# First batch of a three-layer kernel: norms, residue, Newton's steps and mix moved by slots

## The chip, the cores and the metric

The kernel runs on one core of a Trainium2 chip. The metric is the device time in microseconds (us) of one execution; of the kernel before there are three such times, and their median is what a change is held against.

## The reference, cut to what matters

Three layers follow each other: a Nyström attention (8 batches, 8 heads, 576 positions, 64 columns a head), a mixing layer with an MLP, and a Fourier mixing layer with an MLP. The change touches the attention of the first batch.

```python
q_lm = q.reshape(B, H, 32, 18, D).mean(axis=3)      # landmarks, k_lm alike
A, Bm, C = sm(q, k_lm), sm(q_lm, k_lm), sm(q_lm, k)  # softmax of scaled products
Z = Bm.T / (norm1(Bm) * norminf(Bm) + 1e-06)
for _ in range(6):
    Z = 2 * Z - Z @ Bm @ Z                           # Newton's steps
x = A @ Z @ C @ v
u = x + (x.T @ U @ V).T                              # mixing
y = u + relu(u @ w_ch1) @ w_ch2                      # MLP, float64 weights converted on the chip
```

## The kernel before, in words

Everything is written out in a hand-made order, and each engine works through its own list in that order: an instruction that waits holds up all that stand behind it on its engine. What is recorded first comes first.

Before the first MLP there are 21 slots, from `FIRST` = -21 to -1. In each slot the loop runs the steps of the batches that are due in it (`slots.run`), then perhaps `filler(s)`, then some pieces of the weights' conversion (`convs`). A batch's steps and the slots, counted from its own start, are in `Batch.steps`. Batch 0 starts at slot 0 of the 21, batch 1 eleven slots later, so batch 1's `kernel` to `query` lie beside batch 0's `heads`, `rank` and `mix`. Steps of one slot stand in the order of the batches: batch 0's first.

- `landmark` sums 18 rows of k or q on VectorE and scales them into `kb` and `qb`. `landmark_sums` does the same for batch 1's k with 18 products by a unit matrix on TensorE, three to a slot; `filler` places them, and where there are none it issues six products by the unit matrix that nobody reads (12 TensorE instructions, since a product of 32-bit floats runs as two).
- `kernel`, `kernel_norm`, `kernel_t`: the 32x32 softmax, its transpose `BT`, its sums and `dg`. `norms` multiplies `dg` (TensorE), `residue` squares `BT`; six `newton` steps follow, each a product whose result VectorE and ScalarE carry into the next.
- `scores`: products of `qb` and k; VectorE takes their maxima, ScalarE the exponentials `E`. `query(0)`, `query(1)`, `query(2)` are products of q and `kb`, each reduced on VectorE.
- `heads`, `rank` and `mix(g, n)`: the output products. `mix` gives `u1T` in PSUM; ScalarE copies it (line 1014) and for each finished half `hand_head` splits it into a high part `x` (ScalarE, line 50) and a low part (VectorE, line 51). With the four `x` tiles the MLP's first products start (lines 238 to 240, `up`).
- `direct` asks for the raw float64 weights (line 87, SyncE's queue) and converts them (lines 95 to 105 on VectorE, with help of ScalarE and GpSimd). It also decides how early a raw tile is asked for.

Products leave TensorE through PSUM banks taken in turn: `ps_n` 2, `ps_c` 2, `ps_b` 1 for the attention, `ps` 3 for the MLP and the filler (`mlp.bank`). A bank is written again only when what was in it has been read.

Of the kernel before, what the change touches and what calls it, by code (L numbers as in the profile page):

```python
# [22 lines left out]
LM, W = 32, 18  # L23
# [12 lines left out]
def f32(ap):  # L36
    return ap.bitcast(F32)
# [3 lines left out]
def body(ctx: ExitStack, tc: tile.TileContext, qT, kT, vn, mU, mV, w11, w12, w21, w22,  # L41
         ident, bones, istack, tabs, out):
    nc = tc.nc
# [42 lines left out]
    def fetch_raw(raw, src):  # L86
        nc.sync.dma_start(raw, src.bitcast(U32))
# [47 lines left out]
    def rows(d):  # L135
        return slice(d * P, (d + 1) * P)
# [33 lines left out]
    class Mlp:  # L170
# [17 lines left out]
        def fetch(self, nm, src):  # L188
            t = f32(self.weight(nm))
            if isinstance(src, tuple):  # L190
                for n, part in enumerate(src):
                    nc.sync.dma_start(t[:, :, 256 * n:256 * n + 256], part)
            else:
                nc.sync.dma_start(t, src)
# [501 lines left out]
    class Batch:  # L696
# [25 lines left out]
        def landmark(self, nm, g):  # L722

            src, dst = getattr(self, nm)[:, 2 * g:2 * g + 2, :], self.t[nm + "b"]
            s_ = self.pool.tile([P, 2, LM], F32, name="ls", bufs=2)
            nc.vector.tensor_reduce(s_, src.rearrange("p e (m w) -> p e m w", w=W), axis=AX.X, op=ALU.add)
            for j in range(2):
                nc.gpsimd.tensor_scalar_mul(dst[64 * j:64 * j + 64, 2 * g:2 * g + 2, 32 * (j ^ g):32 * (j ^ g) + 32],
                                            s_[64 * j:64 * j + 64], 1.0 / W if nm == "k" else 0.125 / W)

        def landmark_sums(self, nm, first, last):

# [55 lines left out]

        def norms(self):

            ps = self.bank("n" if self.b > 1 else "b")
            nc.tensor.matmul(ps[:, 0:P], self.t["bones"], self.dg.rearrange("p a b -> p (a b)"), start=True, stop=True)
            n = self.stat(4).rearrange("p (g k) -> p g k", k=2)
            nc.vector.tensor_reduce(n.rearrange("p g k -> p (g k)"), ps[:, 0:P].rearrange("p (a b) -> p a b", b=R),
                                    axis=AX.X, op=ALU.max)
            self.c = self.stat(2)
            nc.vector.tensor_tensor(self.c, n[:, :, 0], n[:, :, 1], op=ALU.mult)
            nc.vector.tensor_scalar_add(self.c, self.c, 1e-6)
            nc.vector.reciprocal(self.c, self.c)
# [201 lines left out]
        def mix(self, g, n):  # L1001
            W_, at, u = self.t["W"], self.t["at"], u1[self.b]
            if self.b == 0:
                self.mlp.hand_tail(0, 2 * g + n)
            if n == 0:
                self.u1T = [self.pool.tile([P, S], F32, name="u1T", bufs=UB) for _ in range(2)]
            q = slice(n * HS, (n + 1) * HS)
            pss = [self.bank("n") if not n else self.bank("c") if self.b else self.mlp.bank() for _ in range(2)]
            for c, cl in enumerate(self.EJ):
                for r, sl in enumerate(self.EJ):  # L1010
                    nc.tensor.matmul(pss[r][cl, 0:HS], W_[sl, 2 * g + c, :], at[sl, 2 * g + c, q], start=True,
                                     stop=True)
            for r in range(2):
                nc.scalar.copy(self.u1T[r][:, q], pss[r][:, 0:HS])
            if n == 1:
                for r in range(2):
                    i = 2 * g + r
                    nc.scalar.dma_start(u[rows(i), :], self.u1T[r])
                    self.mlp.hand_head(self.b, i, self.u1T[r])

        def steps(self, after):

            H0, H1 = slice(0, 512), slice(512, 1152)
            a, b = (2, 1) if self.b > 1 else (0, 0)
            yield from ((2 * (nm == "q") + g - a, lambda nm=nm, g=g: self.landmark(nm, g)) for nm in "kq"
                        for g in (0, 1) if (self.b, nm) not in LANDMARKS)
            yield from ((5 - a, self.kernel), (6 - a, self.kernel_norm), (7 - a, self.kernel_t))
            if a:
                yield 6, self.norms
            yield 6, self.scores  # L1030
            if not a:
                yield 8, self.norms
            yield 9 - b, self.residue
            yield from ((10 - b + i, lambda i=i: self.newton(i)) for i in range(6))
            yield from ( (8, lambda: self.query(0)), (9, lambda: self.query(1)),
                        (9, lambda: self.query_exp(H0)), (9, self.scores_sum), (9, lambda: self.query(2)), (10, lambda: self.scores_t(0)),
                        (11, lambda: self.scores_t(1)), (11, self.scores_tail), (11, lambda: self.query_exp(H1)),
                        (11, lambda: self.query_norm(H0)), (12, self.values), (12, lambda: self.query_norm(H1)),
                        (13, lambda: self.query_t(0)), (13, self.query_tail), (14, lambda: self.query_t(1)),
                        (15, self.mixed), (16 - b, self.heads), (17 - b, self.rank))  # L1040
            if self.b:
                yield 13, lambda: self.mlp.get_tail(self.b)
                yield from ((15 + k // 2, lambda k=k: self.mlp.hand_tail(self.b, k)) for k in range(4))
            yield from ((19 + g, lambda g=g, n=n: self.mix(g, n)) for g in range(2) for n in range(2))
            if after:
                yield from ((r, lambda nm=nm: after.load(nm)) for r, nm in ((7, "k"), (10, "q"), (13, "v")))

# [276 lines left out]
    def some(gen, n):  # L1324
        for _ in range(n):
            next(gen, 0)
# [156 lines left out]
    with pool("mm") as mp, pool("pm", space=PSUM) as pm:  # L1483
        mlp = Mlp(mp, pm, 3, passes)

        def direct():

            ws = [mlp.weight(nm) for nm in ("w1", "w2") for _ in range(HM)]
            raws = []
            seq = [*range(4), *range(HM, 2 * HM, 2), *range(4, HM), *range(HM + 1, 2 * HM, 2)]  # L1490

            def fetch():
                i = len(raws)
                if i < len(ws):
                    if i < EARLY:
                        raw = f32(mp.tile([P, 2, 512], F32R, name="g", bufs=HM)).rearrange(
                            "p a n -> p (a n)").bitcast(U32)
                    else:
                        raw = cv0.tile([P, 1024], U32, name="wraw", bufs=2)
                    fetch_raw(raw, srcs[0][seq[i]])  # L1500
                    raws.append(raw)

            for n in range(2):
                fetch()
                yield 1

            old = None
            for n, i in enumerate(seq):
                while len(raws) < min(max(n + 2, min(n + 3, EARLY)), len(ws)):
                    fetch()  # L1510
                new = convert(cv0, raws[n], ws[i], 2)
                for g in (new, old, old, new):
                    if g:
                        yield next(g)
                old = new
            yield from old

        EARLY = 8
        with pool("aa") as ap_, pool("ac") as ac, pool("cv0") as cv0, pool("pt", space=PSUM) as psb:
# [3 lines left out]
            FIRST, GAP = -1 - Batch.LAST, 11  # L1523
# [21 lines left out]
            with tc.manual_schedule():  # L1545
                for what in "kq":
                    batches[0].load(what)
                attention_constants(ac, t)
                small, large = attention_setup(t, ap_, cv0), direct()
                some(small, 1)  # L1550
                some(large, 1)
                batches[0].load("v")
                some(large, 1)
                convs = chained([small, large])
                for s in range(FIRST, 0):
                    slots.run(s)
                    if s - FIRST in (6, *range(10, 20)):
                        filler(s)
                    some(convs, 0 if s < FIRST + 4 else 1 + s % 2)
                later, gen = staging(cv0, 1, 2), mlp.stream(0)  # L1560
                for s in range(N + GAP - 8):
                    if s >= GAP or s in half:
                        next(gen)
                    else:
                        filler(s)
                    slots.run(s)
                    if s < GAP + 13:
                        some(convs, 2)
                        if s == GAP + 12:
                            some(convs, 99)  # L1570
                    else:
                        some(later, 1 if s % 3 == 2 else 2)
                some(later, 999)
                some(gen, 9)
# [120 lines left out]
```

## Time and profile before

| | |
|---|---|
| median of 3 runs | 1786.77 us (1786.47 to 1788.94) |
| the profiled execution | 1789.14 us |
| its span | 1787.4 us |
| busy: TensorE matmul, weight load | 1757.6 us, 1432.7 us |
| busy: VectorE, ScalarE, GpSimd | 1171.2, 735.6, 328.2 us |
| mean granted TensorE clock | 0.997 of full |

The span is the time from the first instruction to the last; 1.74 us of the execution lie outside it. TensorE's busy share is 98%, and what it idles lies almost wholly ahead of the first MLP product. In rows of the time line the columns are start, length (us), engine, line, operation, what is written and read with shapes, count, and in brackets the idle time of the engine ahead of the first one and what ended it; rows of one engine can overlap, since an instruction's record includes its way through the engine.

### The profile page before, as it was taken

The numbers are of one execution on the slowest core, as the hardware profiler recorded it, in microseconds if no ns is written. First come the engines' busy times: TensorE is split into PE (matmuls) and PEld (weight loads), VectorE is DVE, ScalarE is ACT, GpSimd is POOL, SyncE is SP. The second block draws the span as 40 slices with busy tenths as digits, with TensorE's granted clock in tenths as the row PEclk, the third lists the DMA queues.
The fourth block names the chain that finished last, engine by engine and source line by source line (L and its number), as shares of the span: only waits on it lengthen the run. The fifth ranks groups of instructions, "written<-read, shape, count | busy, mean of one in ns | idle before, by whom it ended". The sixth has DMA issues, their size and how long they took to land.

```text
span 1787.4 us, 30912 instructions
## 1 busy us (share of the span) xinstructions
PE 1757.6 (98%) x11905; PEld 1432.7 (80%) x11905; DVE 1171.2 (66%) x2028; ACT 735.6 (41%) x1520; POOL 328.2 (18%) x314
## 2 busy tenths in 40 slices
PE   6999999999999999999999999999999999999999
PEld 4777777777788888888878888888878888888887
DVE  7897666566322977888886665657575674577564
ACT  4554443444211333433342333434256445454642
POOL 3324211221110321211111122211111001100100
PEclk9999999999999999999999999999999999999999
DMA  7555456443536764546555954776688778878764
GB/s 254 182 174 171 152 175 206 155 162 105 179 137 249 242 234 154 183 164 216 179 179 193 329 200 148 273 281 201 222 290 273 216 243 257 261 228 247 223 214 153
DMA packets 215895, 371.00 MB, mean 208 GB/s; under 512 B 28970, under 2 KB 129930, under 8 KB 215748
## 3 DMA queue, kind: packets, MB, share of 16 engines
q1 hardware_dynamic: 211140, 359.59, 60.9%
q10 hardware_dynamic: 4608, 9.44, 1.4%
q8 instruction: 94, 1.54, 0.4%
q14 instruction: 53, 0.43, 0.1%
HBM read 262.18 MB, written 106.17 MB: 206 GB/s over the span
## 4 chain that ended last, share of the span: by engine, by line
PE 88%; DVE 7%; DMA 2%; ACT 1%; issue 1%; SPq 0%; POOL 0%; DVEq 0%; ACTq 0%
PE ps L291 9%; PE ps L293 9%; PE ps L292 9%; PE ps L238 9%; PE ps L240 8%; PE ps L239 8%; PE ps L329 7%; PE ps L331 7%; PE ps L330 7%; PE ps L554 1%; PE ps L553 1%; PE ps L555 1%; PE ps_f L77 1%; PE ps_f L76 1%; PE ps_f L75 1%
## 5 line engine op out<-in xcount | busy, mean ns | idle before, releaser
L238 PE MATMUL ps<-x,w 128*128 128x512 f32 x768 | 305.4, 398 | 0.2 <-DVE g L243 0.2
L291 PE MATMUL ps<-g,w 128*128 128x512 f32 x768 | 304.2, 396 | 0.0
L240 PE MATMUL ps<-x,w 128*128 128x512 f32 x768 | 299.8, 390 | 0.0
L293 PE MATMUL ps<-g,w 128*128 128x512 f32 x768 | 299.8, 390 | 0.0
L239 PE MATMUL ps<-x,w 128*128 128x512 f32 x768 | 299.4, 390 | 0.0
L292 PE MATMUL ps<-g,w 128*128 128x512 f32 x768 | 299.2, 390 | 0.0
L243 DVE SCALAR_TENSOR_TENSOR g<-ps,g 128x512 fp32r<-128x512 f32 x192 | 132.4, 690 | 206.7 <-ACT g L242 206.4
L242 ACT ACTIVATE g<-ps 128x512 fp32r<-128x512 f32 x192 | 114.0, 597 | 264.0 <-PE ps L240 263.4
L291 PEld LDWEIGHTS ps<-g,w 128*128 128x128 f32 x768 | 144.3, 188 | 31.9 <-issue 3.5
L240 PEld LDWEIGHTS ps<-x,w 128*128 128x128 f32 x768 | 144.1, 188 | 31.4
L293 PEld LDWEIGHTS ps<-g,w 128*128 128x128 f32 x768 | 144.1, 188 | 31.1
L238 PEld LDWEIGHTS ps<-x,w 128*128 128x128 f32 x768 | 144.3, 188 | 29.9 <-DVE g L243 0.6
L292 PEld LDWEIGHTS ps<-g,w 128*128 128x128 f32 x768 | 144.4, 188 | 27.4
L239 PEld LDWEIGHTS ps<-x,w 128*128 128x128 f32 x768 | 144.4, 188 | 26.9
L302 DVE TENSOR_TENSOR xf<-ps,xf 128x512 f32<-128x512 f32 x88 | 60.5, 687 | 86.7 <-PE ps L293 84.6
L406 ACT COPY ps<-ps 128x512 f32<-128x512 f32 x126 | 72.4, 575 | 94.4 <-PE ps L331 93.4
L51 POOL TENSOR_TENSOR stg<-cva,stg 128x512 fp32r<-128x512 f32 x48 | 65.4, 1363 | 216.8 <-ACT stg L50 190.4
L458 POOL TENSOR_TENSOR w<-w,w 128x512 f32<-128x512 f32 x24 | 33.3, 1389 | 362.1 <-DMA w<-rs 181.6
L329 PE MATMUL ps<-xs,w 128*128 128x512 f32 x240 | 94.2, 392 | 1.9 <-ACT ps L406 1.9
L331 PE MATMUL ps<-xs,w 128*128 128x512 f32 x240 | 94.1, 392 | 0.0
L330 PE MATMUL ps<-xs,w 128*128 128x512 f32 x240 | 93.9, 391 | 0.0
L51 POOL TENSOR_TENSOR x<-xf,x 128x512 fp32r<-128x512 f32 (+7 forms) x48 | 60.1, 1254 | 157.9 <-ACT x L50 122.7
(420 smaller groups left out, 3356.9 us busy)
## 6 DMA issues: line engine op xcount, KB each, us to landing
w<-e SPq DMA_DIRECT2D x84, 512.0 KB
w<-d SPq DMA_DIRECT2D x126, 256.0 KB
w<-d SPq DMA_DIRECT2D x60, 512.0 KB
wraw<-w SPq DMA_DIRECT2D x56, 512.0 KB
d<-stg SPq DMA_DIRECT2D x48, 512.0 KB
y<-xf SPq DMA_DIRECT2D x64, 256.0 KB
xf<-y SPq DMA_DIRECT2D x52, 256.0 KB
u<-u1T ACTq DMA_DIRECT2D x32, 288.0 KB
```

The lines of the kernel that those rows point to most:

```text
L51: (eng or nc.vector).tensor_tensor(lo, src, f32(hi), op=ALU.subtract)
L238: nc.tensor.matmul(ps, wh, xh, start=k == 0, stop=False)
L239: nc.tensor.matmul(ps, wl, xh, start=False, stop=False)
L240: nc.tensor.matmul(ps, wh, xl, start=False, stop=k == 3)
L242: nc.scalar.activation(g[:, 0, :], ps, AF.Relu)
L243: nc.vector.scalar_tensor_tensor(out=g[:, 1, :], in0=ps, scalar=0.0, in1=f32(g[:, 0, :]), op0=ALU.max, op1=ALU.subtract)
L291: nc.tensor.matmul(ps, wh, gh, start=k == m0, stop=False)
L292: nc.tensor.matmul(ps, wl, gh, start=False, stop=False)
L293: nc.tensor.matmul(ps, wh, gl, start=False, stop=k == m1 - 1)
L329: nc.tensor.matmul(ps, wh, xh, start=first and k == 0, stop=False, skip_group_check=True)
L330: nc.tensor.matmul(ps, wl, xh, start=False, stop=False, skip_group_check=True)
L331: nc.tensor.matmul(ps, wh, xl, start=False, stop=last and k == 1, skip_group_check=True)
```

## The change

For batch 0 alone (`e` is 1 there, else 0): `kernel_t` moves from slot 7 to 6, `norms` from 8 to 7, `residue` from 9 to 8, Newton's six steps, `heads` and `rank` one slot forward, and `mix` from slots 19 and 20 to 17 and 18. `norms` takes a `ps_n` bank instead of `ps_b`; all four banks of a `mix(g, .)` pair come from the MLP's three. The landmarks of batch 0 are scaled on ScalarE instead of GpSimd. Slots 17 and 18 have no filler any more. The second raw weight tile is asked for after batch 1's k instead of ahead of it.

```diff
-                nc.gpsimd.tensor_scalar_mul(dst[...], s_[64 * j:64 * j + 64], 1.0 / W if nm == "k" else 0.125 / W)
+                (nc.gpsimd.tensor_scalar_mul if self.b else nc.scalar.mul)(
+                    dst[...], s_[64 * j:64 * j + 64], 1.0 / W if nm == "k" else 0.125 / W)
...
-            ps = self.bank("n" if self.b > 1 else "b")
+            ps = self.bank("b" if self.b == 1 else "n")
...
-            pss = [self.bank("n") if not n else self.bank("c") if self.b else self.mlp.bank() for _ in range(2)]
+            pss = [self.mlp.bank() if not self.b else self.bank("c" if n else "n") for _ in range(2)]
...
-            a, b = (2, 1) if self.b > 1 else (0, 0)
+            a, b = (2, 1) if self.b > 1 else (0, int(not self.b))
+            e = int(not self.b)
-            yield from ((5 - a, self.kernel), (6 - a, self.kernel_norm), (7 - a, self.kernel_t))
+            yield from ((5 - a, self.kernel), (6 - a, self.kernel_norm), (7 - a - e, self.kernel_t))
-                yield 8, self.norms
+                yield 8 - e, self.norms
-            yield from ((19 + g, lambda g=g, n=n: self.mix(g, n)) for g in range(2) for n in range(2))
+            yield from ((19 - 2 * e + g, lambda g=g, n=n: self.mix(g, n)) for g in range(2) for n in range(2))
...
-            for n in range(2):
-                fetch()
-                yield 1
+            fetch()
+            yield 1
...
                 batches[0].load("v")
-                some(large, 1)
...
-                    if s - FIRST in (6, *range(10, 20)):
+                    if s - FIRST in (6, *range(10, 17), 19):
```

Three places show what the numbers do to the order. First TensorE, at the start of batch 0; its `kernel` products stand ahead of these rows. `dg,bones_sb` is `norms`, `BT` the residue, `kb,q` with `ps_c` is `query(0)` and then `query(1)`, with `ps_b` `query(2)`, `ry` a Newton step. Before:

```order
L1543 MATMUL ps<-ident_sb 128x128 x6
L792 MATMUL ps_b<-dg,bones_sb 128x128
L896 MATMUL ps_c<-kb,q__229 32x64 x32
L806 MATMUL ps_n<-BT 32x32 x8
L896 MATMUL ps_c<-kb,q__229 32x64 x32
L903 MATMUL ps_b<-kb,q__229 32x64 x8
L969 MATMUL ps_n<-ry 32x64 x8
L851 MATMUL ps_c<-ident_sb,E 128x128 x4
```

Now, on the same engine at the same place:

```order
L1544 MATMUL ps<-ident_sb 128x128 x6
L793 MATMUL ps_n<-dg,bones_sb 128x128
L807 MATMUL ps_n<-BT 32x32 x8
L897 MATMUL ps_c<-kb,q__229 32x64 x32
L970 MATMUL ps_n<-ry 32x64 x8
L897 MATMUL ps_c<-kb,q__229 32x64 x32
L904 MATMUL ps_b<-kb,q__229 32x64 x8
L970 MATMUL ps_n<-ry 32x64 x8
L852 MATMUL ps_c<-ident_sb,E 128x128 x4
```

The residue now stands ahead of `query(0)`, the first Newton step ahead of `query(1)`, and the second where the first one stood.

Second ScalarE, from the first of batch 0's mix or batch 1's scores on (`E` are batch 1's exponentials, `u1T` and `x` batch 0's mix, `w_260` a converted weight). Before:

```order
L837 ACTIVATE E,st<-ps_c,st 128x512
L839 ACTIVATE E,st<-ps_b,st 128x64
L837 ACTIVATE E,st<-ps_c,st 128x512
L839 ACTIVATE E,st<-ps_n,st 128x64
L50 CAST w_260<-cva 128x512
L100 ACTIVATE g<-g 128x512
L1014 COPY u1T<-ps_n 128x288 x2
L1014 COPY u1T<-ps 128x288 x2
L1018 DMA u_0_58<-u1T 128x576
L50 CAST x<-u1T 128x512
L1018 DMA u_0_58<-u1T 128x576
L50 CAST x<-u1T 128x512
```

Now:

```order
L1015 COPY u1T<-ps 128x288 x4
L1019 DMA u_0_58<-u1T 128x576
L50 CAST x<-u1T 128x512
L1019 DMA u_0_58<-u1T 128x576
L50 CAST x<-u1T 128x512
L838 ACTIVATE E,st<-ps_c,st 128x512
L840 ACTIVATE E,st<-ps_b,st 128x64
L838 ACTIVATE E,st<-ps_c,st 128x512
L840 ACTIVATE E,st<-ps_n,st 128x64
L50 CAST w_260<-cva 128x512
L1015 COPY u1T<-ps 128x288 x4
L1019 DMA u_0_58<-u1T 128x576
```

Before, both halves of the mix stand behind the exponentials; now the first stands ahead of them and the second behind.

Third VectorE in the same slots (`st<-ps_c`, `st<-ps_b`, `st<-ps_n` are the maxima of batch 1's scores, `BT` and `dg` its `kernel_t`, `x<-u1T,x` the low parts of batch 0's mix). Before:

```order
L831 TENSOR_REDUCE st<-ps_c 128x1 x2
L833 TENSOR_REDUCE st<-ps_b 128x1
L833 TENSOR_REDUCE st<-ps_n 128x1
L834 TENSOR_TENSOR st<-st 128x2
L782 STREAM_TRANSPOSE BT<-ry 128x64
L783 TENSOR_REDUCE st<-BT 128x2
L785 TENSOR_TENSOR dg<-istack_sb,st 128x128
L99 TENSOR_SCALAR cvp<-cva 128x512
L102 SCALAR_TENSOR_TENSOR cvp<-g,cvp 128x512
L95 TENSOR_SCALAR cva<-g 128x512
L96 SCALAR_TENSOR_TENSOR cva<-g,cva 128x512
L51 TENSOR_TENSOR x<-u1T,x 128x512 x2
```

Now:

```order
L51 TENSOR_TENSOR x<-u1T,x 128x512 x2
L774 TENSOR_SCALAR st<-st 128x2
L775 RECIPROCAL st<-st 128x2
L778 TENSOR_TENSOR ry<-sB,st 128x2x32
L779 TENSOR_TENSOR st<-st 128x2
L832 TENSOR_REDUCE st<-ps_c 128x1 x2
L834 TENSOR_REDUCE st<-ps_b 128x1
L834 TENSOR_REDUCE st<-ps_n 128x1
L835 TENSOR_TENSOR st<-st 128x2
L51 TENSOR_TENSOR x<-u1T,x 128x512 x2
L783 STREAM_TRANSPOSE BT<-ry 128x64
L784 TENSOR_REDUCE st<-BT 128x2
```

The first two low parts now stand ahead of batch 1's `kernel_norm` and maxima, the other two between the maxima and `kernel_t`.

## Rows read from the trace of the kernel before

**Rows 1.** Stretches: length, each engine's busy time (count), clock, DMA share, GB/s.
```profile
58.00:160.00 102.00, 99.72 (x1217) 75.29 (x1215) 87.79 (x172) 53.96 (x136) 42.07 (x42) 1.00 0.51 169
160.00:1787.00 1627.00, 1617.22 (x9837) 1326.21 (x9835) 1038.43 (x1749) 655.32 (x1314) 268.80 (x242) 1.00 0.63 209
```

**Rows 2.** Time line of TensorE, the start.
```profile
13.69 2.35 PE L1543 MATMUL ps<-ident_sb 128*128 128x128 f32 x12
19.59 0.41 PE L903 MATMUL ps_b<-kb,q__229 128*32 128x64 f32 x16
23.75 0.65 PE L969 MATMUL ps_n<-ry 32*32 32x64 f32 x16 [3.75 <-DVE cva L95]
```

**Rows 3.** Waits between 18 and 24 us: us in total, times, longest.
```profile
PEld ps_n L969 <- issue: 3.9, 1, 3.9
```

**Rows 4.** DMA queues from 20 to 24 us: packets, MB, share of 16 engines.
```profile
q1 hardware_dynamic: 377, 1.46, 97.5%
q8 instruction: 1, 0.02, 1.7%
```

**Rows 5.** Stretches at the start, columns as in Rows 1.
```profile
0.00:19.99 19.99, 8.35 (x222) 5.97 (x222) 13.57 (x33) 4.62 (x15) 5.86 (x19) 1.00 0.87 305
22.10:28.90 6.80, 5.15 (x49) 4.49 (x50) 5.82 (x14) 1.97 (x5) 1.32 (x1) 0.50 0.79 273
```

**Rows 6.** Time line of TensorE, from batch 0's last steps to the MLP.
```profile
39.77 1.68 PE L738 MATMUL ps<-k__372,ident_sb 128*128 128x128 f32 x6
42.84 1.60 PE L1543 MATMUL ps<-ident_sb 128*128 128x128 f32 x12
...
45.86 2.94 PE L1543 MATMUL ps<-ident_sb 128*128 128x128 f32 x24
...
50.92 0.65 PE L1011 MATMUL ps_n<-at,W 64*64 64x288 f32 x3 [1.49 <-ACT E L839]
...
52.24 0.49 PE L792 MATMUL ps_b<-dg,bones_sb 128*128 128x128 f32 x2
52.66 1.10 PE L896 MATMUL ps_c<-kb,q__510 128*32 128x64 f32 x64
53.69 1.60 PE L1543 MATMUL ps<-ident_sb 128*128 128x128 f32 x12
55.22 0.72 PE L1011 MATMUL ps_n<-at,W 64*64 64x288 f32 x8
...
56.44 0.33 PE L806 MATMUL ps_n<-BT 32*32 32x32 f32 x16
...
57.95 0.50 PE L238 MATMUL ps<-x,w 128*128 128x512 f32 x1
```

**Rows 7.** Time line of ScalarE, batch 1's exponentials and batch 0's mix.
```profile
48.83 0.69 ACT L837 ACTIVATE E<-ps_c,st 128x512 f32<-128x512 f32 x1 [3.44 <-PE ps L1543]
...
51.26 0.70 ACT L100 ACTIVATE g<-g 128x512 f32<-128x512 f32 x1
51.84 0.70 ACT L1014 COPY u1T<-ps_n 128x288 f32<-128x288 f32 x2
```

**Rows 8.** Time line of VectorE in the same slots.
```profile
46.26 0.17 DVE L773 TENSOR_SCALAR st<-st 128x2 f32<-128x2 f32 x1
...
48.58 0.16 DVE L834 TENSOR_TENSOR st<-st 128x2 f32<-128x2 f32 x1
48.66 0.24 DVE L782 STREAM_TRANSPOSE BT<-ry 128x64 f32<-128x64 f32 x1
...
49.39 0.42 DVE L99 TENSOR_SCALAR cvp<-cva 128x512 uint32<-128x512 uint32 x1
...
53.91 1.29 DVE L51 TENSOR_TENSOR x<-u1T,x 128x512 fp32r<-128x512 f32 x2 [2.31 <-ACT x L50]
...
58.05 1.29 DVE L51 TENSOR_TENSOR x<-u1T,x 128x512 fp32r<-128x512 f32 x2
59.26 0.40 DVE L809 SCALAR_TENSOR_TENSOR ry<-ps_n,st,istack_sb 128x32 f32<-128x32 f32 x2
```

More of the change, by code (lines that the diff above doesn't have):

```diff
@@ L727, in landmark @@
             for j in range(2):
-                nc.gpsimd.tensor_scalar_mul(dst[64 * j:64 * j + 64, 2 * g:2 * g + 2, 32 * (j ^ g):32 * (j ^ g) + 32],
-                                            s_[64 * j:64 * j + 64], 1.0 / W if nm == "k" else 0.125 / W)
+                (nc.gpsimd.tensor_scalar_mul if self.b else nc.scalar.mul)(
+                    dst[64 * j:64 * j + 64, 2 * g:2 * g + 2, 32 * (j ^ g):32 * (j ^ g) + 32],
+                    s_[64 * j:64 * j + 64], 1.0 / W if nm == "k" else 0.125 / W)
         def landmark_sums(self, nm, first, last):
```

## The prediction

> **What bounds the kernel now.** The page comes first: TensorE is busy almost all the time, so the question is where it is not. The busy times by stretch answer that. From 160 us on it works 1617.22 of 1627 us; from 58 to 160 us it lacks 102 - 99.72 = 2.28 us [rows 1]. All that the change touches lies ahead of the first MLP product, which starts at 57.95 us [rows 6]. So the time is that start plus a fixed amount of TensorE work, less what of the 2.28 us a late TensorE no longer has to wait for.
>
> The second view is TensorE's time line of the first 58 us. Its first stop that counts ends at 23.75 us, after 3.75 us [rows 2]. The reason is not in the bracket: the wait list puts 3.9 us of the weight load's wait down to "issue", that is to no semaphore [rows 3], and in that stretch one packet of the instruction queue passes among data that fill 97.5% of the DMA engines [rows 4]. I read it as the next piece of program arriving late. It comes after 222 TensorE instructions [rows 5], a place in the program and not in the work. The clock then stands at 0.50, that is 1.2 GHz, from 22.1 to 28.9 us [rows 5]. From 23.75 to the end of the last landmark sums (39.77 + 1.68 = 41.45 us) TensorE has no gap worth a row.
>
> The third view is the time lines of ScalarE and VectorE in batch 0's last slots. There the two hand work to each other in the written order: VectorE's maxima of batch 1's scores (end 48.74) let ScalarE start the exponentials (48.83), these and two conversion pieces stand ahead of the mix's copies (51.84), and VectorE stands 2.31 us until the first high part of x is there (53.91) [rows 7, 8].
>
> **The change, part by part.**
>
> *Batch 0's start.* Landmarks on ScalarE, `kernel_t` ahead of the maxima, the residue ahead of `query(0)`, the first Newton step ahead of `query(1)`: all of it lies ahead of the stop at instruction 222. Counting the new order (16 for kernel, 32 scores, 12 filler, 2 norms, 16 residue, 64 query(0), 16 Newton, 64 query(1)) gives 222 at the last product of `query(1)`. So the stop now stands between `query(1)` and `query(2)`, and whatever is won ahead of it waits there. I cost these edits at 0 up to the stop; if the stop were gone the cover would be gone too (a rival below). What is left of the gain: behind the stop stands `query(2)` (0.41 us) instead of the first Newton step (0.65 us) [rows 2], -0.2 us. The later raw tile moves 512 KB behind batch 1's k in a queue that stays full; the bytes asked for ahead of the stop are the same, so 0, between -1 us (the program comes sooner) and +1.
>
> *Rank to mix.* From the stop to the end of the landmark sums TensorE did 41.45 - 23.75 = 17.7 us without a gap; now the same less 0.2, so to 41.25 us. Rank now fits into the wait of batch 1's `kernel` for `kb`, which with the kernel takes 42.84 - 41.45 = 1.39 us; then the remaining filler, 1.60 us [rows 6]. The first mix starts at 44.2 us, against 48.7 to 50.9 before. Gone are 24 unread products (2.94 us) and a wait of 1.49 us for a bank [rows 6]. This is the intended gain, and it is real up to here.
>
> *What it is then tied to.* The first two low parts of x now stand on VectorE ahead of batch 1's `kernel_norm` and maxima. From the start of a mix to the end of its second low part the trace has 59.34 - 55.22 = 4.12 us [rows 6, 8]; the fourth bank of a mix now waits for a copy out of the three, about 0.2 us more (my estimate from one copy of 0.70/2 us [rows 7]). So 44.2 + 4.3 = 48.5 us. Then `kernel_norm` and maxima, 46.26 to 48.74, 2.48 us [rows 8], and 0.1 to ScalarE: the exponentials start at 51.1, where before they started at 48.83. Behind them on ScalarE stand a conversion piece and the second mix's copies: 51.26 - 48.83 = 2.43 us [rows 7], so copies at 53.5. From the copies to the second low part: 55.20 - 51.84 = 3.36 [rows 7, 8], with 0.2 for the bank 57.1 us. Only then comes `kernel_t`, which before ran straight behind the maxima: 49.39 - 48.66 = 0.73 us [rows 8], so `dg` at 57.85 and TensorE's norms at 57.9, where before they ran at 52.24. Behind norms on TensorE, in order, stand `query(0)`, the filler of slot 19, the residue, `query(1)`, `query(2)`: 55.22 - 52.24 = 2.98 and 57.95 - 56.44 = 1.51, together 4.49 us [rows 6]. The MLP starts at 62.4 instead of 57.95: +4.4 us.
>
> *The clock.* TensorE now has little to do from about 47 us (mix, scores, half of the second mix) to 57.9. Before, 3.75 us of idling ended in 1.2 GHz, and that lasted until 28.9, 5 us after work came back [rows 2, 5]. Twelve unread products took 2.35 us at the slow start and 1.60 later [rows 2, 6]. With the same factor of about 1.4 the 4.49 us become 6.3, and the MLP starts at 64.2: +6.2 us. The Trainium skill ("TensorE: Matmul & The Clock Gate", "What's actually happening") says that the slow clock is the default and activity releases it; that speaks against taking fillers out just where TensorE begins to wait, and the trace agrees by its 0.50 after the stop.
>
> *What comes back.* VectorE is the other full engine: 87.79 of 102 us after 58 [rows 1]. From `dg` it still has 51.60 - 49.39 = 2.2 us of conversion and 58.05 - 55.20 = 2.85 us of norms, query and conversion before its residue (59.26) [rows 8], so that comes at 62.8: +3.5 us. TensorE's waits after 58 us are waits for VectorE's lag, so a TensorE that is 4.4 to 6.2 late with a VectorE 3.5 late gets back something, at most 2.28. The end lies between +3.5 and +6.2; I take the middle, +4.8. The profiled execution of 1789.14 us (1.74 outside the span) would become 1793.9; it lies 2.37 over the median of the runs, so the median goes to 1786.77 + 4.8 = 1791.6 us.
>
> **Rivals.**
>
> *The last product of `query(1)` is caught behind the stop, or the stop ends later.* Then two reductions and subtractions more stand on VectorE behind it, about 1.5 us, near the 1.29 us of a pair of its instructions of that width [rows 8], and the slow clock reaches into the MLP. +6.5 us, 1793.3. For it: the count ends exactly there. Against it: VectorE has slack of the same size ahead of the first low part.
>
> *The stop goes.* Fewer tiles asked for, the program comes in time, the clock stays at 2.4 GHz. TensorE could go on at 20.7, 3 us sooner, and win some 1.6 us of the 5.15 done at 1.2 GHz [rows 5]; but VectorE has its own list in that stretch and lets less through, and I allow about half of the 4.6, 2.5 us. All later steps move by it: MLP at +1.9 to +3.7, end at about +1.8, 1788.6. Against it: the same bytes are in the queue. The Trainium skill ("Runtime: NRT & Kernel Launch", "Instruction fetch mechanics") calls the cost of going to the next block of program "mostly hidden". By that rule this would be the case at hand, at 1788.6; the trace has 3.75 us at this place before, and the measurement decides.
>
> *The mix does not hold VectorE: faster.* If the second low parts were ready when VectorE comes to them, `kernel_t` would follow the maxima as before, and the 2.94 + 1.49 us would be won: about -3.5 us, the rest lying on VectorE's own work, 1783.3. It decides at VectorE's wait ahead of the second pair of low parts: under 1 us it is this case, by the sum above it is 57.1 - 1.3 - 51.0, about 4.8 us. Against it stands the written order of both engines.
>
> **How the numbers follow.** 0.60 for the forecast (its own range 1789.9 to 1793), 0.14 for the later stop, 0.15 for no stop, 0.11 for the faster case (half of it only partly so, and then within the bound). About 0.2% (3.6 us) is what a measurement of this kernel can tell from no change. Slower by more: most of the forecast and all of the first rival, some 0.66. Within: the rest of the forecast, the second rival, half of the last: 0.27. Faster: 0.07. The range leaves out the full gain and the upper end of the first rival: 1785.5 to 1794.
>
> **What would show it.** Right: no long gap on TensorE ahead of the first Newton step but one ahead of `query(2)` of like size; first mix near 44 us; ScalarE's exponentials of batch 1 near 51; VectorE idle for 4 us or more ahead of the second pair of low parts; norms of batch 1 near 58, at 0.50 clock; first MLP product at 62 to 64. Wrong: the MLP's first product before 60 us, a wait at the second low parts under 1 us, or a late MLP start that the total doesn't show because VectorE sets the pace after it.

## The result and the profile after

The changed kernel takes 1798.4 us (median of 4 runs, 1797.1 to 1799.0) against 1786.6 us before: a ratio of 1.0059, interval 1.0047 to 1.0072, or 8 to 13 us more. The forecast was 1791.6 us; the direction was right, the size less than half of the measured one. In the profiled execution (1798.85 us, span 1797.1) the first MLP product comes at 68.68 us instead of 57.95, 10.73 us later.

TensorE's time line, start of batch 0 (start, length, engine, line, operation, count, idle time ahead and what ended it):

```profile
18.34 0.42 PE L970 MATMUL ps_n<-ry 32*32 32x64 f32 x16
18.70 1.09 PE L897 MATMUL ps_c<-kb,q__229 128*32 128x64 f32 x63
23.32 0.26 PE L897 MATMUL ps_c<-kb,q__229 128*32 128x64 f32 x1 [3.52 <-issue]
...
36.22 0.38 PE L937 MATMUL ps_b<-ident_sb,A 128*64 128x128 f32 x2 [1.50 <-DVE A L923]
...
41.99 1.68 PE L739 MATMUL ps<-k__376,ident_sb 128*128 128x128 f32 x6
```

VectorE behind that last product of `query(1)`:

```profile
23.62 0.69 DVE L909 TENSOR_REDUCE sm<-ps_c 128x16 f32<-128x512 f32 x1 [3.43 <-PE ps_c L897]
```

The residue and the first Newton step ran ahead of the stop, as the change wants. But the stop [rows 2] now falls before the 64th of `query(1)`'s products, not behind it. VectorE, which before worked through it, stands 3.43 us, and TensorE later waits 1.50 us for VectorE's part of the same queries (`query_tail`). The landmark sums end at 43.67 us instead of 41.45 [rows 6].

TensorE from there to the MLP:

```profile
46.52 2.08 PE L1012 MATMUL ps<-at,W 64*64 64x288 f32 x16
48.53 1.09 PE L824 MATMUL ps_c<-k__376,qb 64*32 64x512 f32 x16
...
56.78 1.23 PE L1012 MATMUL ps<-at,W 64*64 64x288 f32 x6 [5.94 <-ACT u1T L1015]
61.59 0.80 PE L793 MATMUL ps_b<-dg,bones_sb 128*128 128x128 f32 x2 [3.57 <-DVE dg L786]
62.32 1.94 PE L897 MATMUL ps_c<-kb,q__522 128*32 128x64 f32 x64
64.18 2.93 PE L1544 MATMUL ps<-ident_sb 128*128 128x128 f32 x12
...
68.68 0.50 PE L238 MATMUL ps<-x,w 128*128 128x512 f32 x1
```

VectorE, then ScalarE, in the same slots:

```profile
50.13 1.40 DVE L51 TENSOR_TENSOR x<-u1T,x 128x512 fp32r<-128x512 f32 x2 [1.71 <-ACT x L50]
...
59.50 1.29 DVE L51 TENSOR_TENSOR x<-u1T,x 128x512 fp32r<-128x512 f32 x2 [5.71 <-ACT x L50]
60.71 0.24 DVE L783 STREAM_TRANSPOSE BT<-ry 128x64 f32<-128x64 f32 x1
...
67.55 0.41 DVE L810 SCALAR_TENSOR_TENSOR ry<-ps_n,st,istack_sb 128x32 f32<-128x32 f32 x2 [0.22 <-PE ps_n L807]
```

```profile
53.89 0.69 ACT L838 ACTIVATE E<-ps_c,st 128x512 f32<-128x512 f32 x1 [3.08 <-DVE st L835]
...
56.31 0.72 ACT L1015 COPY u1T<-ps 128x288 f32<-128x288 f32 x2
58.06 0.70 ACT L1015 COPY u1T<-ps 128x288 f32<-128x288 f32 x2 [1.03 <-PE ps L1012]
```

This is the chain of the forecast: low parts (end 51.53), maxima, exponentials (53.89), second mix (56.31), its low parts (60.79), `kernel_t`, norms (61.59). On it the three engines wait in turn: VectorE 1.71 and 5.71 us, ScalarE 3.08 and 1.03, TensorE 5.94 and 3.57. Before, `kernel_t` followed the maxima at 48.66 [rows 8].

The stretches tell the rest (length, busy time of TensorE's products, weight load, VectorE, ScalarE, GpSimd, then clock, DMA share, GB/s):

```profile
49.00:61.60 12.60, 3.08 (x49) 1.08 (x33) 5.57 (x17) 7.15 (x20) 1.29 (x1) 0.69 0.64 229
58.00:68.70 10.70, 7.13 (x178) 6.34 (x175) 8.06 (x19) 4.24 (x8) 2.03 (x2) 0.56 0.15 57
68.68:160.00 91.32, 88.91 (x1142) 67.89 (x1135) 81.14 (x161) 47.05 (x116) 35.33 (x36) 1.00 0.52 173
```

TensorE worked 3.08 of 12.6 us; in the stretch behind, the granted clock is 0.56 on average, near its 1.2 GHz level, so `query(0)` takes 1.94 us instead of 1.10 and the unread products 2.93 instead of 1.60 [rows 6]. From the first MLP product to 160 us TensorE idles 2.41 us; before it was 2.28 from 58 us [rows 1].

What becomes of the late start is read from the same products further on. Three rows of the changed kernel:

```profile
175.49 0.50 PE L238 MATMUL ps<-x,w 128*128 128x512 f32 x1
...
246.73 0.47 PE L897 MATMUL ps_c<-kb,q__2685 128*32 128x64 f32 x18 [0.53 <-issue]
...
642.67 0.50 PE L238 MATMUL ps<-x,w 128*128 128x512 f32 x1 [1.13 <-DVE g L243]
```

The first is the product that before starts so:

```profile
165.49 0.50 PE L238 MATMUL ps<-x,w 128*128 128x512 f32 x1
```

There the changed kernel is 10.0 us late, 0.7 less than at the first MLP product. At before's 236.59 us it is 10.8 late again, at 630.52 us 12.2: the kernel before has neither of the two waits shown.

### The profile page after: what moved, and what is told of

Same layout as the page of the kernel before. It is cut to its first block, busy times and chain, and to the rows that moved or that the text cites. A ratio compares the mean times of both kernels' runs of the same rounds, so it can differ in the third digit from the quotient of the medians.

```text
span 1797.1 us, 30863 instructions
## 1 busy us (share of the span) xinstructions
PE 1757.9 (98%) x11881; PEld 1431.9 (80%) x11881; DVE 1173.7 (65%) x2028; ACT 738.1 (41%) x1528; POOL 326.9 (18%) x306
## 4 chain that ended last, share of the span: by engine, by line
PE 86%; DVE 7%; DMA 4%; ACT 2%; issue 1%; SPq 1%; POOL 0%; ACTq 0%; DVEq 0%
PE ps L291 9%; PE ps L238 8%; PE ps L293 8%; PE ps L292 8%; PE ps L240 8%; PE ps L239 8%; PE ps L329 7%; PE ps L331 7%; PE ps L330 7%; DMA d<-stg 1%; PE ps L555 1%; PE ps L554 1%; PE ps L553 1%; PE ps_f L76 1%; PE ps_f L77 1%
```

## The experiments

The ratios are to the kernel before, timed beside each of the others (medians of 1786.62 to 1787.86 us). The lag is that of the first MLP product in the profiled execution, against before's 57.95 us. It comes from one execution of each kernel: six of these kernels are ordered like before up to the end of the landmark sums (mix alone, TensorE alone later and the last four), and there those sums end between 0.94 us sooner and 0.69 us later than in before. So a lag is good to about 1 us.

| | ratio, interval | lag, us |
|---|---|---|
| the change | 1.0059 [1.0047, 1.0072] | 10.73 |
| mix put back | 1.0022 [1.0014, 1.0031] | 2.80 |
| mix alone | 1.0055 [1.0043, 1.0068] | 10.80 |
| splits of x later | 1.0026 [1.0017, 1.0035] | 3.64 |
| five unread | 1.0045 [1.0031, 1.0058] | 9.22 |
| busy gap | 1.0046 [1.0033, 1.0059] | 11.11 |
| TensorE alone later | 1.0037 [1.0024, 1.0050] | 6.30 |
| raw tiles behind q | 1.0009 [1.0000, 1.0018] | 2.10 |
| mix put back, five | 1.0009 [1.0000, 1.0018] | 1.49 |
| mix between | 1.0018 [1.0009, 1.0027] | 3.14 |
| the same, unread kept | 1.0001 [0.9993, 1.0010] | 1.77 |
| the same, second in 20 | 1.0017 [1.0008, 1.0026] | 1.86 |
| rearranged | 1.0002 [0.9993, 1.0011] | -2.13 |

**The mix put back, and the mix alone.** On the changed kernel, and on the kernel before:

```diff
-            yield from ((19 - 2 * e + g, lambda g=g, n=n: self.mix(g, n)) for g in range(2) for n in range(2))
+            yield from ((19 + g, lambda g=g, n=n: self.mix(g, n)) for g in range(2) for n in range(2))
...
-                    if s - FIRST in (6, *range(10, 17), 19):
+                    if s - FIRST in (6, *range(10, 20)):
```
```diff
-            pss = [self.bank("n") if not n else self.bank("c") if self.b else self.mlp.bank() for _ in range(2)]
+            pss = [self.mlp.bank() if not self.b else self.bank("c" if n else "n") for _ in range(2)]
...
-            yield from ((19 + g, lambda g=g, n=n: self.mix(g, n)) for g in range(2) for n in range(2))
+            yield from ((19 - 2 * int(not self.b) + g, lambda g=g, n=n: self.mix(g, n)) for g in range(2) for n in range(2))
...
-                    if s - FIRST in (6, *range(10, 20)):
+                    if s - FIRST in (6, *range(10, 17), 19):
```

> The changed kernel with batch 0's two mixes put back to slots 19 and 20 and the unread products of slots 10 to 19 put back; the sooner norms, residue and Newton's steps, the evictions on ScalarE, the MLP's banks and the later raw tiles stay. Theory (the loss is the mix moved in among batch 1's maxima and exponentials, which makes VectorE's chain wait for ScalarE and back again): 1786 to 1789, at most the 2 us that the stop inside query(1) costs remain. Rival (the loss comes from the start, the stop and the raw tiles, and is passed on): 1792 or more.

> The kernel before with batch 0's mixes alone moved to slots 17 and 18 (in the MLP's banks, no unread products in those two slots). Theory (the mix's place is the loss): 1793 to 1796, about +8. Rival (the mix is hidden, the loss comes from the other parts): 1786 to 1788.

Measured: 1791.75 and 1798.52 us. The mix alone is as slow as the whole change: 9.8 us by the ratio (7.7 to 12.2), where I expected about 8; its median lies 2.5 us above my range. Without the mix some 4 us remain: the first time lies between theory and rival, just short of the rival's 1792. The parts don't add up, 10.80 and 2.80 against 10.73. The first mix starts at 46.52 us in the change and at 45.91 in the mix alone, but their first low parts end level (51.53 and 51.70): from there on both go through the same chain, so what the stop cost the change ahead of them no longer shows. VectorE of the mix alone:

```profile
50.39 1.31 DVE L51 TENSOR_TENSOR x<-u1T,x 128x512 fp32r<-128x512 f32 x2 [3.69 <-ACT x L50]
...
59.80 1.29 DVE L51 TENSOR_TENSOR x<-u1T,x 128x512 fp32r<-128x512 f32 x2 [5.71 <-ACT x L50]
```

**The splits of x later.** The changed kernel, with batch 0's splits taken out of `mix`:

```diff
...
-                    self.mlp.hand_head(self.b, i, self.u1T[r])
+                    if self.b:
+                        self.mlp.hand_head(self.b, i, self.u1T[r])
...
+            if not self.b:
+                yield from ((19 + i // 2, lambda i=i: self.mlp.hand_head(0, i, self.us[i])) for i in range(4))
```

> The changed kernel, but batch 0's splits of x into high and low parts go to slots 19 and 20; the mix's products and their eviction with the residue stay in 17 and 18. So VectorE's low parts no longer stand ahead of batch 1's maxima and norms. Theory (the price of the mix is VectorE's low parts waiting for ScalarE's high parts ahead of the maxima and the norms): 1787 to 1791. Rival (the price is TensorE's, its clock and the stop, whatever VectorE's order): 1796 to 1799.

Measured: 1792.86 us, a lag of 3.64 instead of 10.73 us. So 7.1 us of the lag lie in the place of the splits, ScalarE's high parts and VectorE's low parts, ahead of the maxima; the time is 2 us above the expected range and well below the rival's. Of what was left two parts show on TensorE: the second mix still waits 3.56 us for a bank whose copy stands behind the exponentials, and `query(0)` still takes 1.94 us, as at the slow clock.

```profile
53.98 1.23 PE L1013 MATMUL ps<-at,W 64*64 64x288 f32 x6 [3.56 <-ACT u1T L1016]
55.14 0.79 PE L793 MATMUL ps_b<-dg,bones_sb 128*128 128x128 f32 x2
55.86 1.94 PE L897 MATMUL ps_c<-kb,q__522 128*32 128x64 f32 x64
```

**Five unread products instead of six in slot 6,** on the changed kernel, and on the one with the mix put back:

```diff
-                for _ in range(6):
+                for _ in range(5 if s - FIRST == 6 else 6):
```

> The changed kernel with five instead of six unread products in slot 6, so that four fewer instructions of TensorE stand before its stop and the stop falls behind query(1)'s last product instead of ahead of it. Theory (the stop holds that product, VectorE waits for it and passes some 2.3 us on to the first MLP product): 1795.5 to 1796.5. Rival (the landmark sums' lag is swallowed later): 1798.4, no difference.

> The changed kernel with the mixes put back to slots 19 and 20 and five instead of six unread products in slot 6: what is left of the change is the sooner norms, residue and Newton's steps, the evictions on ScalarE, the MLP's banks and the later raw tiles, without the stop ahead of query(1)'s last product. Theory (of the first MLP product's 2.8 us that are left without the moved mix, the stop is all but the mix's wait for a bank): 1788 to 1789.5, 2 to 3 below the kernel with the mixes alone put back. Rival (the raw tiles or the evictions cost as well): 1791 or more.

Measured: 1796.50 and 1788.93 us, both as the theory has it. The stop stays (3.31 us), but behind `query(1)`; here in the first of the two:

```profile
19.01 1.10 PE L897 MATMUL ps_c<-kb,q__229 128*32 128x64 f32 x64
19.93 0.22 PE L904 MATMUL ps_b<-kb,q__229 128*32 128x64 f32 x1
23.46 0.43 PE L904 MATMUL ps_b<-kb,q__229 128*32 128x64 f32 x15 [3.31 <-issue]
```

Each pair alone has overlapping intervals; both move by the same 2 to 3 us, and the lag by 1.5 and 1.3. The landmark sums show it most clearly: in the four kernels whose stop falls ahead of that product (the change, mix put back, splits later, busy gap) they end between 43.18 and 44.32 us, in these two at 41.65 and 41.89. Two products fewer, four instructions with their weight loads, that compute nothing decide on which side of a product the stop falls. In the second kernel TensorE begins batch 1's scores at 44.74 us, level with before (44.73); most of its last 1.5 us comes from a further wait put down to "issue" among these products (0.32 us) and their slower run, whose cause no run shows. What the evictions on ScalarE and the later raw tiles cost one by one was not tested; with the sooner start they are within this kernel's 0 to 3.2 us.

**A busy gap.** The changed kernel with unread products where TensorE stood idle:

```diff
-                for _ in range(6):
+                for _ in range({17: 22, 18: 12}.get(s - FIRST, 6)):
...
-                    if s - FIRST in (6, *range(10, 17), 19):
+                    if s - FIRST in (6, *range(10, 20)):
```

> The changed kernel with 22 unread products between batch 1's scores and the first mix and 12 ahead of the norms' products, so that TensorE has work in the gap in which its clock fell to 0.5. Theory (the clock's fall, which makes query(0) and the norms' products take twice their time, is 3 us of the loss): 1795 to 1796. Rival (VectorE and ScalarE pace that stretch and the clock is a consequence only): 1798 or more.

Measured: 1795.4 us, as the theory has it, but the interval overlaps the change's, and the profiled execution was the slowest of its five (1800.6). In it the norms' products take 0.49 us again and from there to the MLP it is 69.06 - 63.03 = 6.03 us instead of 7.09, while `dg` comes 1.4 us later. In this stretch the slow clock cost 1.1 us at least, the difference of the two, and 7.09 - 4.49 = 2.6 us at most; how much of it the whole time has isn't settled.

**TensorE alone later.** The kernel before, with 24 unread products in slot 20:

```diff
-                for _ in range(6):
+                for _ in range(24 if s - FIRST == 20 else 6):
...
-                    if s - FIRST in (6, *range(10, 20)):
+                    if s - FIRST in (6, *range(10, 21)):
```

> The kernel before with 24 unread products right ahead of the first MLP product, on TensorE alone: some 6 us of its time, while VectorE and ScalarE go on as before. Tests by itself what a later first MLP product costs at the end. Theory (TensorE has hardly any idle time behind it, so it is passed on): 1792 to 1793. The prediction's step (up to 2.3 us of idle time behind it take some of it back): 1790 to 1791.

Measured: 1794.52 us, above both ranges; by the ratio 6.6 us more, 4.3 to 8.9 by the interval. TensorE, then VectorE:

```profile
58.87 5.62 PE L1543 MATMUL ps<-ident_sb 128*128 128x128 f32 x48
64.25 0.48 PE L238 MATMUL ps<-x,w 128*128 128x512 f32 x1
...
170.46 0.50 PE L238 MATMUL ps<-x,w 128*128 128x512 f32 x1
```
```profile
67.90 0.69 DVE L243 SCALAR_TENSOR_TENSOR g<-ps,g 128x512 fp32r<-128x512 f32 x1 [4.10 <-ACT g L242]
```

VectorE is not held up ahead of the MLP, but behind its first product it stands 4.10 us until TensorE's result has come through ScalarE, so it can't run ahead for long. In the trace the step of the prediction is there at first: of the 6.30 us, 4.97 are left at the product that before starts at 165.49 us, so 1.3 came back. From 630 us on they are lost again, and the spans differ by 6.6 us. The interval allows both readings, the whole lag and the lag less 1.4.

**Raw tiles behind q.** The kernel before, with raw tiles 1 to 3 asked for behind batch 1's q (the first two loads of `direct` and the loop's `fetch` moved):

```diff
-            for n in range(2):
-                fetch()
-                yield 1
+            fetch()
+            yield 1
...
                 new = convert(cv0, raws[n], ws[i], 2)
+                if not n:
+                    yield next(new)
+                while len(raws) < min(max(n + 2, min(n + 3, EARLY)), len(ws)):
+                    fetch()
...
```

> The kernel before with batch 1's query tiles asked for ahead of raw tiles 1 to 3. Tests whether TensorE's stop near 20 us, whose instruction fetch stands in the DMA queues, depends on how much data was asked for ahead. Theory (it waits behind the data): the stop shrinks from 3.75 to below 1.5 us and the time to 1784 to 1785. Rival (it does not depend on the order of the requests): 3.5 to 3.8 us of stop, 1786.6.

Measured: 1788.53 us; neither this time nor the length of the stop is what theory or rival expected. The stop halved: it ends 1.15 us sooner, and TensorE reaches it 0.71 later. VectorE paid for it, waiting for a raw tile. TensorE, then VectorE, then the DMA queues from 17 to 20 us:

```profile
22.60 0.43 PE L969 MATMUL ps_n<-ry 32*32 32x64 f32 x16 [1.89 <-DVE sm L908]
```
```profile
29.59 0.43 DVE L95 TENSOR_SCALAR cva<-g 128x512 uint32<-128x512 uint32 x1 [3.76 <-DMA g<-w]
```
```profile
q1 hardware_dynamic: 244, 0.99, 93.6%
q8 instruction: 1, 0.02, 2.5%
```

The instruction packet that before passed after 20 us [rows 4] now passes ahead of it. In the traces' records of that packet (16 KB) it runs from 21.17 to 22.28 us before, 20.75 to 21.84 in the changed kernel and 19.89 to 21.11 here, and the stop ends at 23.75, 23.32 and 22.60: each time 1.47 to 1.49 us behind the packet. In all fourteen traces it is 1.3 to 1.6 us. So the stop is the program's next piece; that this waits behind data is what the one run shows.

**The mix between.** Four kernels from the one before, to see whether a sooner mix can pay in another order. The first mix goes to slot 18, behind batch 1's scores; the exponentials go behind its copies, the low parts stay in 19 and 20:

```diff
+            if self.b == 1:
+                yield 7, self.scores_exp
...
-            yield from ((19 + g, lambda g=g, n=n: self.mix(g, n)) for g in range(2) for n in range(2))
+            yield from (((19 + g) if self.b else (18, 19)[g], lambda g=g, n=n: self.mix(g, n)) for g in range(2) for n in range(2))
+            if not self.b:
+                yield from (((19, 20)[i // 2], lambda i=i: self.low(i)) for i in range(4))
...
-                    if s - FIRST in (6, *range(10, 20)):
+                    if s - FIRST in (6, *range(10, 17), 19):
...
```

The second keeps the unread products of slot 18 too, the third has `(18, 20)`. The fourth takes `norms` out of the bank that the exponentials free, and lets batch 1's steps call batch 0's splits and second mix:

```diff
-            ps = self.bank("n" if self.b > 1 else "b")
+            ps = self.bank("n" if self.b else "b")
...
+            if self.b == 1:
+                yield from ((8, lambda i=i: self.mlp.first.low(i)) for i in range(2))
...
+            yield 8, lambda: self.query(0)
+            if self.b == 1:
+                yield from ((8, lambda n=n: self.mlp.first.mix(1, n)) for n in range(2))
...
```

> The kernel before with batch 0's mixes one slot sooner, not two: in slots 18 and 19, behind batch 1's scores on TensorE, with batch 1's exponentials put behind the first mix's eviction on ScalarE and the low parts of x left in slots 19 and 20 on VectorE; the MLP's banks, no unread products in slots 17 and 18. Nothing on VectorE's chain of maxima and norms then waits for a mix. Theory (the loss of the change is the order, not the earlier mix itself): the first MLP product comes 2 to 3 us sooner than before's 57.95, and that is passed on: 1784 to 1785. Rival (an earlier mix costs by itself, through the clock or the banks): 1787 to 1790.

> The same with 12 instructions of unread products left in slot 18, between the two mixes. If TensorE's clock falls in the gap without them, this is the faster of the two by the 1 to 3 us that the slow products cost; if not, it is the same within 1 us.

> The same as the kernel with the mixes in slots 18 and 19, but the second mix stays in slot 20, behind batch 1's query(0), so that the norms' products don't stand behind a mix that waits for a bank. Theory (the bank wait of the second mix is on the path to the norms): 1783 to 1784.5. Rival (VectorE is later than that wait anyway): the same as with slots 18 and 19.

> The kernel before, rearranged by what the runs so far show: batch 0's first mix in slot 18 behind batch 1's scores, its splits of x behind batch 1's norms, the second mix behind batch 1's query(0), batch 1's norms in the third tag's bank so that they don't wait for the exponentials, and 12 instructions of unread products between the first mix and the norms. Theory (what the first MLP product waits for is only the order on VectorE and ScalarE and the two banks): it comes at 55.5 to 56.5 us and the time is 1.5 to 2.5 below the kernel before. Rival (the work of VectorE itself is the bound there, whatever the order): within 1 us of the kernel before.

Measured: 1790.81, 1788.47, 1790.13 and 1787.53 us. My theory for the first and the third missed: all three start the MLP later than before, not sooner, and moving the second mix alone changes little, as the rival had it. The second mix's bank wait is 4.24 us in the first; in the third the norms wait 4.04 us for the exponentials to free their bank; in all three the clock falls. Between the first two, the unread products are worth 2.3 us of the medians and 1.4 of the lag, though the intervals just touch. It isn't the clock that they save: it stands at 0.50 for 3.4 us in both. In the traces 0.5 of the 1.4 is there already ahead of the first mix, and the second mix waits 2.20 us for its bank instead of 4.24. The fourth cuts the first of these waits to 0.94 us, is rid of the second, and starts the MLP at 55.82 us, as expected, with the clock full. Part of that is luck: its landmark sums, which the edit doesn't touch, end 0.94 us sooner than before's.

```profile
49.60 0.49 PE L792 MATMUL ps_n<-dg,bones_sb 128*128 128x128 f32 x2 [0.56 <-DVE dg L785]
50.52 1.10 PE L903 MATMUL ps_c<-kb,q__510 128*32 128x64 f32 x64 [0.42 <-ACT E L845]
...
55.82 0.50 PE L238 MATMUL ps<-x,w 128*128 128x512 f32 x1
```

Its time is that of before. By 768 us its MLP has gone from 2.13 us sooner to 0.39 later. TensorE's waits from 58 to 800 us, in the fourth and then in before (total, times, longest):

```profile
PE ps_b L943 <- DVE A L929: 2.4, 3, 1.2
PE ps_l L1277 <- DVE le L1272: 1.4, 1, 1.4
PE ps L238 <- DVE g L243: 1.0, 2, 0.6
PE ps_c L903 <- issue: 0.9, 1, 0.9
```
```profile
PE ps_l L1255 <- DVE le L1250: 1.4, 1, 1.4
PE ps_b L936 <- DVE A L922: 1.0, 3, 0.6
PE ps_n L969 <- issue: 0.8, 1, 0.8
```

What the start wins, 2.4 us of waits for VectorE take back (1.4 more in `query_tail`, 1.0 new in the MLP); the waits put down to "issue" are level. In eleven of the twelve late rows of the table the lag lies within the interval of the time lost (the busy gap is the exception), so a late TensorE pays about its lag. The one early start gained nothing that the times show. No version here beats the kernel before.

## Why the prediction was wrong in size

*The step that failed* is the sum that puts the first MLP product at 64.2 us. It took the stop at 0, the wait for a fourth bank at 0.2 us each time and the slow clock at a factor of 1.4. Measured, these make the first product 4.5 us later than forecast, 68.68 us. What was to come back of that did not show in the total.

*The frame held* roughly: the end is the MLP's start plus a nearly fixed amount of work. The lag is 10.73 us at the first product, 10.0 at before's 165.49 us, 10.8 at 236.59 and 12.7 at 1289.15. The spans differ by 9.7 us only because before's profiled execution then lost time of its own near 1322 us, where its clock stands at 0.50 for 3.4 us; its 1789.14 us lie above the median for that. TensorE's idle time is less one-sided than I had it: of the 29.8 us before, 17.3 lie ahead of the first MLP product and 12.5 behind it.

*The stop* was costed at 0, "whatever is won ahead of it waits there". The count to instruction 222 was right but for one product: 221 stand ahead of the stop, and the last of `query(1)` behind it. I took just this for a rival at 0.14 and let VectorE's slack speak against it. It happened: 43.67 - 41.25 = +2.42 us at the landmark sums, and the two kernels that move the stop by four instructions get most of it back. The rival that the stop goes did not happen: 3.52 us. The Trainium skill ("Runtime: NRT & Kernel Launch", "Instruction fetch mechanics") has this cost "mostly hidden"; here it shows in every trace, 1.89 us at the least.

*Rank to mix* held: 46.52 - 43.67 = 2.85 us against 2.95.

*The tie* held as a mechanism; the runs with the mix alone and with the splits later show it. Its links were mostly sized right: low parts to exponentials 2.36 us (2.58 forecast), to the copies 2.42 (2.43), low parts to norms 0.80 (0.8). Two were not: mix to low parts 5.01 (4.3) and copies to low parts 4.48 (3.56). Both hold the wait for a fourth bank out of the MLP's three, which I took at 0.2: ScalarE must copy, TensorE fill, ScalarE copy again. Between the two pairs of copies lie 1.22 and 1.75 us here. Together -0.22 - 0.01 + 0.71 + 0.92 = +1.40.

*The clock* had the right sign; 4.49 us became 7.09, not 6.3: +0.79. TensorE has no gap in these 7.09 us. The factor of 1.4 was too small: the twelve unread products that it came from took 2.35 us at before's start, but 2.93 us at 64.18 here, 1.83 times the 1.60.

*The sum* at the first MLP product: 6.2 + 2.42 - 0.10 + 1.40 + 0.79 = 10.7 us, the measured lag.

*What comes back* was taken as the middle between VectorE's lag and TensorE's, +3.5 and +6.2. Measured, VectorE's residue is 8.3 us late (67.55 us against 59.26 [rows 8]) and TensorE 10.7; the middle is 9.5, and the lag is 10.0 at before's 165.49 us. So far the step held, and so it did in the run with TensorE alone later. But in both traces later waits took it away again, and the whole times can't tell the full lag from one that is 1.4 us shorter. Whether anything comes back for good stays open.

*The faster case* was to be decided at VectorE's second wait, under 1 us or about 4.8. It was 5.71.

## What to carry to other kernels

Before an item is moved sooner in a written order, follow each engine it hands to: what stands behind it there now waits for its last step, and the price is the round trip, not the item's length. Ahead of an engine that is busy to the end, a lag at the start was paid about whole here and the one lead was lost to the next engine's pace, so such a change risks more than it can win. A stop at a fixed place in the program should be counted to the instruction, with both sides of a borderline priced.

## What the hardware showed that was not expected

The program's next piece arrived late near 20 us in every kernel run here, and the stop ended 1.3 to 1.6 us behind its packet in all fourteen traces. With the raw tiles asked for behind q the packet came 1.2 us sooner, and the stop was 1.89 us long instead of 3.75.

Some of VectorE's operations took much longer while GpSimd was at work. VectorE in the rearranged kernel, then GpSimd:

```profile
45.92 1.04 DVE L777 TENSOR_TENSOR ry<-sB,st 128x64 f32<-128x64 f32 x1
...
50.98 1.65 DVE L96 SCALAR_TENSOR_TENSOR cva<-g,cva 128x512 uint32<-128x512 uint32 x1
```
```profile
45.59 1.28 POOL L51 TENSOR_TENSOR w<-cva,w 128x512 fp32r<-128x512 f32 x1 [2.56 <-ACT w L50]
...
50.69 1.40 POOL L103 TENSOR_TENSOR cvp<-cvp,cva 128x512 f32<-128x512 f32 x1 [3.82 <-DVE cvp L102]
```

The first takes 0.22 us in before, where GpSimd is idle then, and the second 0.69 elsewhere. Both end shortly behind the operation of GpSimd under which they began (46.96 behind 46.87, 52.63 behind 52.09). The Trainium skill ("GPSIMD Engine Reference", "1. Specifications") says that GpSimd shares its way into SBUF with VectorE, and that an operation of VectorE with two inputs there contends for it; these two have two, and the trace agrees. GpSimd's first operation comes 5.9 us sooner here than before, since ScalarE's cast of the same weight now stands ahead of the exponentials; so a change of ScalarE's order put 0.8 us onto VectorE's chain. No run tested it by itself.
